# The first layer of experts 1 to 7 as seven block products (Strassen's algorithm, one level)

## The chip, the cores and the metric

The kernel runs on one core of a Trainium2 chip. The core has TensorE (PE, with its weight loads as PEld), VectorE (DVE), ScalarE (ACT), GpSimd (POOL) and SyncE (SP), each with its own queue of instructions. The metric is the time of one execution in device microseconds: 835.72 us, median of three runs (833.84 to 838.47).

## The reference

Attention over a sliding window, then a layer of eight experts, of which each token takes two:

```python
def _attn_ref(q, k, v, n_sink, window):          # 4 batches, 8 heads, 768 positions, 64 wide
    scores = scale * np.matmul(q, k.transpose(0, 1, 3, 2))
    keep = is_sink | in_window                   # 4 sinks, window of 128
    scores = np.where(keep, scores, -1000000000.0)
    a = softmax(scores)
    return np.matmul(a, v)
...
def _moe_ref(x, w_gate, w_noise, noise, w1, w2): # x 3072 x 512, w1 8 x 512 x 1024, w2 8 x 1024 x 512
    noisy_logits = x @ w_gate + np.log1p(np.exp(x @ w_noise)) * noise
    top2, top2_w = the two best experts of each token, and their softmax
    for e in range(E):
        for k in range(2):
            mask = top2[:, k] == e
            h = np.maximum(x[mask] @ w1[e], 0.0)
            out[mask] += top2_w[mask, k, None] * (h @ w2[e])
```

The change is to `x[mask] @ w1[e]`.

## The kernel before

**Numbers.** All is float32. For TensorE a matrix is split into two parts of a narrower type (float32r): a high part, which is a rounded copy written by ScalarE, and a low part, which is the difference and is written by VectorE (`minus`, L191 and L192). One product is three matmuls, high by high, high by low and low by high.

**Order.** A planner (`Plan`, L44) takes every operation with its engine, an assumed duration, a priority and the buffers that it reads and writes. It simulates the engines and writes out one fixed order for each. A tag with a ring of n buffers can be ahead of its readers by n. Phase one is attention of four batches with the routing of each; phase two is the routing of the last batch and then the experts.

**Experts.** Each expert has 832 slots for tokens, in seven tiles: six of 128 and a last one (TF) of 64 (R). Before, an expert is worked in two pieces, tiles 0 to 2 (384 columns) and tiles 3 to 6 (448 columns); expert 0 has 512 and 320. F is 1024, in 8 blocks f of 128. For each piece and each f:

- `up` (L990): twelve matmuls, four blocks of the 512 inputs by three, into a bank H (two of them). These are L997 to L999: w1 is stationary, the tokens stream.
- `up_h` (L1008, ScalarE) writes the rectified high part, `up_l` (L1015, VectorE) the low part.
- `down` (L1018) for each tile of the piece: three matmuls of 512 columns into the tile's bank Y (L1026 to L1028), for the last tile two (L1031, L1032).

So first and second layer alternate, f by f. When a tile's bank Y is complete, ScalarE scales it by the routing weight (L1035; the last tile takes `half`, `whole` and `scaled`), and GpSimd adds it to the output by an indirect DMA (`scatter`, L1048 to L1052, with a one-element memset ahead of it).

**Inputs of an expert.** `w_chunk` (L918) brings each matrix in four chunks of 512 KB: SP loads a chunk into one of two staging buffers `st`, ScalarE writes the high part (L940), VectorE the low part (L944). A chunk of w1 serves two blocks f. `gather` (L825, L838) brings the tokens, 32 rows by each of 26 indirect DMAs of GpSimd into a ring `xg` of five buffers; a gate (`after`) ties gathers to the f of the piece before. `weight` (L964) copies the routing weights, four 32 x 1 copies a tile. `rows_turn` (L868) turns a tile with VectorE's transpose of 32 x 32 blocks (L886) and splits it, high by ScalarE (L895), low by VectorE, into `skn` and `sqn`, two buffers each.

The first layer's matmuls in the kernel before:

```python
for i in range(DC):
    xh, xl = (x[:, i, :width] for x in both)
    nc.tensor.matmul(p, w[:, 0, i], xh, start=(i == 0), stop=False)
    nc.tensor.matmul(p, w[:, 0, i], xl, start=False, stop=False)
    nc.tensor.matmul(p, w[:, 1, i], xh, start=False, stop=(i == DC - 1))
```

## Time and profile before

| | |
|---|---|
| time, median of three runs | 835.72 us |
| profiled execution, span | 836.0 us |
| granted clock of TensorE, mean | 0.990 |
| matmuls in the profile | 4801 |
| `up`, L997 to L999, all experts | 512 each, 541.4 us busy in sum |
| gathers (L838) | 182, 180.6 us of GpSimd |
| scatters (L1050) | 56, 92.0 us of GpSimd |
| data moved | 97.10 MB, mean 116 GB/s |

"Busy" is the time from the start of an instruction to its end, and instructions of one engine that overlap are counted once in the shares but each for itself in the groups. A row of a group reads: line, engine, operation, output <- input, count, then busy time, mean ns of one, then the engine's idle time just before them and what ended it. "Issue" is idle time for which the profile names no releaser. A row of the timeline reads: start, length, engine, line, operation, tile and, in brackets, the wait ahead of it.

### The profile page before, as it was taken

The numbers are of one execution on the slowest core, as the hardware profiler recorded it, in microseconds if no ns is written. First come the engines' busy times: TensorE is split into PE (matmuls) and PEld (weight loads), VectorE is DVE, ScalarE is ACT, GpSimd is POOL, SyncE is SP. The second block draws the span as 40 slices with busy tenths as digits, with TensorE's granted clock in tenths as the row PEclk, the third lists the DMA queues.
The fourth block names the chain that finished last, engine by engine and source line by source line (L and its number), as shares of the span: only waits on it lengthen the run. The fifth ranks groups of instructions, "written<-read, shape, count | busy, mean of one in ns | idle before, by whom it ended". The sixth has DMA issues, their size and how long they took to land.

```text
span 836.0 us, 13410 instructions
## 1 busy us (share of the span) xinstructions
PE 794.0 (95%) x4801; PEld 668.6 (80%) x4801; DVE 442.8 (53%) x1094; ACT 343.5 (41%) x677; POOL 430.3 (51%) x601
## 2 busy tenths in 40 slices
PE   6999997898899799999999999999999999999996
PEld 3776775676677589888988988898899889889984
DVE  5878979888673334346335424633542463454220
ACT  4876785675521323234233323423332341433210
POOL 6555866767416325472753647275364627526212
PEclk9999999999999899999999999999999999999999
DMA  6749886644544186175444617544461654444123
GB/s 120 154 96 226 181 204 183 157 127 100 141 132 131 31 224 165 29 152 120 94 84 127 136 31 153 122 92 84 129 131 35 150 124 94 80 130 78 21 31 47
DMA packets 151750, 97.10 MB, mean 116 GB/s; under 512 B 100704, under 2 KB 129376, under 8 KB 151680
## 3 DMA queue, kind: packets, MB, share of 16 engines
q1 hardware_dynamic: 137744, 67.93, 31.8%
q0 software_dynamic: 13936, 28.27, 19.4%
q8 instruction: 39, 0.64, 0.3%
q14 instruction: 31, 0.25, 0.1%
HBM read 67.44 MB, written 28.72 MB: 115 GB/s over the span
## 4 chain that ended last, share of the span: by engine, by line
PE 75%; issue 7%; DVE 6%; POOL 4%; DMA 4%; ACT 2%; another core or an unknown queue 1%; SPq 1%; POOLq 0%; DVEq 0%; ACTq 0%
PE H L997 10%; PE H L999 10%; PE H L998 10%; PE Y L1026 9%; PE Y L1028 9%; PE Y L1027 9%; PE S L307 4%; PE X L388 2%; PE T L280 2%; PE X L391 2%; POOL out L1050 2%; PE P L365 1%; PE Y L1031 1%; PE Y L1032 1%; DMA st<-in_moe_w 1%
## 5 line engine op out<-in xcount | busy, mean ns | idle before, releaser
L1050 POOL DMA_INDIRECT out<-y,idx x56 | 92.0, 1642 | 241.2 <-ACT y L1035 209.3
L838 POOL DMA_INDIRECT xg<-x_rows,rt_idq x182 | 180.6, 992 | 55.5 <-issue 53.4
L1015 DVE SCALAR_TENSOR_TENSOR h<-H,h 128x384 fp32r<-128x384 f32 (+2 forms) x192 | 79.4, 441 | 219.6 <-ACT h L1008 142.2
L997 PE MATMUL H<-skn,w 128*128 128x448 f32 (+3 forms) x512 | 181.6, 355 | 1.8 <-issue 1.8
L999 PE MATMUL H<-skn,w 128*128 128x448 f32 (+3 forms) x512 | 180.5, 353 | 1.5 <-issue 1.5
L998 PE MATMUL H<-sqn,w 128*128 128x448 f32 (+3 forms) x512 | 179.3, 350 | 1.8 <-issue 1.8
L1008 ACT ACTIVATE h<-H 128x448 fp32r<-128x448 f32 (+3 forms) x128 | 66.1, 516 | 273.7 <-PE H L999 161.8
L997 PEld LDWEIGHTS H<-skn,w 128*128 128x128 f32 x512 | 96.2, 188 | 11.2 <-issue 3.1
L998 PEld LDWEIGHTS H<-sqn,w 128*128 128x128 f32 x512 | 96.3, 188 | 10.6 <-issue 2.4
L999 PEld LDWEIGHTS H<-skn,w 128*128 128x128 f32 x512 | 96.3, 188 | 7.3 <-issue 1.8
L1026 PE MATMUL Y<-w2b,h 128*128 128x512 f32 x192 | 76.0, 396 | 0.3 <-ACT h L1008 0.2
L1028 PE MATMUL Y<-w2b,h 128*128 128x512 f32 x192 | 75.5, 393 | 0.5 <-DVE h L1015 0.5
L1026 PE MATMUL Y<-w2a,h 128*128 128x512 f32 x192 | 75.5, 393 | 0.0
L1027 PE MATMUL Y<-w2b,h 128*128 128x512 f32 x192 | 75.5, 393 | 0.0
L1027 PE MATMUL Y<-w2a,h 128*128 128x512 f32 x192 | 75.0, 391 | 0.0
L1028 PE MATMUL Y<-w2a,h 128*128 128x512 f32 x192 | 74.8, 389 | 0.0
L307 PE MATMUL S<-kq 64*128 64x264 f32 (+1 forms) x384 | 57.4, 410 | 4.4 <-DVE cbuf L317 2.5
L192 POOL TENSOR_TENSOR cbuf<-cbuf,mn 128x528 f32<-128x528 f32 x48 | 51.7, 1077 | 18.4 <-DVE mn L327 16.4
L895 ACT ACTIVATE skn<-xtn 128x512 fp32r<-128x512 f32 (+1 forms) x49 | 29.4, 600 | 68.0 <-DVE xtn L886 55.3
L1028 PEld LDWEIGHTS Y<-w2b,h 128*128 128x128 f32 x192 | 36.3, 189 | 9.9 <-DVE h L1015 1.7
L307 PEld LDWEIGHTS S<-kq 64*128 64x128 f32 x384 | 31.4, 192 | 15.6 <-issue 4.8
L192 DVE TENSOR_TENSOR sqn<-xtn,skn 128x512 fp32r<-128x512 f32 (+1 forms) x49 | 31.9, 652 | 22.1 <-ACT skn L895 16.0
(191 smaller groups left out, 1362.7 us busy)
## 6 DMA issues: line engine op xcount, KB each, us to landing
st<-in_moe_w SPq DMA_DIRECT2D x36, 512.0 KB
st<-in_moe_w SPq DMA_DIRECT2D x112, 128.0 KB
out<-zt SPq DMA_DIRECT2D x31, 256.0 KB
vn<-in_v SPq DMA_DIRECT2D x16, 384.0 KB
x_rows<-xr SPq DMA_DIRECT2D x48, 128.0 KB
kn<-in_k SPq DMA_DIRECT2D x30, 192.0 KB
qn<-in_q SPq DMA_DIRECT2D x30, 192.0 KB
xg<-x_rows,rt_idq POOLq DMA_INDIRECT x182
```

The costliest lines, as they stand in the source:

```text
L192: eng.tensor_tensor(out, a, b, op=OP.subtract)
L307: nc.tensor.matmul(p[:, :2 if j else 1], kq(g)[r, j // 2, 2 + j % 2, NS:], x[:, :2 if j else 1], start=True, stop=True)
L838: nc.gpsimd.indirect_dma_start(out=x[:, i, :], out_offset=None, in_=xbuf.rearrange("r (q d) -> (r q) d", d=sh.SW), in_offset=bass.Indirect ...
L997: nc.tensor.matmul(p, w[:, 0, i], xh, start=(i == 0), stop=False)
L998: nc.tensor.matmul(p, w[:, 0, i], xl, start=False, stop=False)
L999: nc.tensor.matmul(p, w[:, 1, i], xh, start=False, stop=(i == DC - 1))
L1008: nc.scalar.activation(get("h", FC * q + f, [128, 2 * 128 * FIRST], F32R)[:, :width], get("H", FC * q + f), AF.Relu)
L1015: nc.vector.scalar_tensor_tensor(h[:, o:o + s1 - s0], p[:, s0:s1], 0.0, h[:, s0:s1].bitcast(F32), op0=OP.max, op1=OP.subtract)
L1026: nc.tensor.matmul(p, hh, w[:, 0], start=(f == 0), stop=False)
L1027: nc.tensor.matmul(p, hh, w[:, 1], start=False, stop=False)
L1028: nc.tensor.matmul(p, hl, w[:, 0], start=False, stop=(f == FC - 1))
L1050: d = nc.gpsimd.indirect_dma_start(out=out, out_offset=bass.IndirectOffsetOnAxis(ap=c["idx"][:size(e, t), e, t:t + 1], axis=0), in_=get("y ...
```

## The change

Experts 1 to 7 compute the first layer by Strassen's algorithm. Of a pair of blocks f (f0 = 2i and f1 = 2i + 1, with chunk i of w1; i from 0 to 3), the weights are four blocks: the two halves of the 512 inputs by f0 and f1. The tokens are four as well: the halves of the inputs by the halves of the tokens, alternate runs of 32 of the slots, 416 columns each. Instead of eight products of blocks there are seven, a to g, of sums of blocks. Each product is two blocks of 128 inputs by three matmuls, six matmuls of 416 columns. Expert 0 keeps the old way.

```diff
+def split_seven(plan, nc, e, i, n, z):
...
+    def two(b, m, src):
...
+        plan.op("ACT", .06 + .21 * m, z, lambda: nc.scalar.activation(h(), src(), AF.Copy), ...)
+        plan.op("DVE", .06 + .27 * m, z, lambda: minus(v, l(), src(), h().bitcast(F32)), ...)
...
+    two(0, 2, raw)
+    sums(lambda: v.tensor_tensor(extra(), raw(0, 2, 1), raw(2, 4, 1), op=OP.add))
+    sums(lambda: minus(v, raw(0, 2, 1), raw(0, 2), raw(0, 2, 1)))
+    two(6, 1, extra)
+    two(2, 2, lambda: raw(0, 4, 1))
+    sums(lambda: minus(v, raw(0, 2), extra(), raw(0, 2)))
+    sums(lambda: minus(v, raw(2, 4), raw(2, 4), raw(0, 2)))
+    two(4, 2, raw)
...
+def rows_seven(plan, nc, sh, e, t, size, z):
...
+    def sums(o, a, b):
+        plan.op("Pool", .33 * f, z, lambda: minus(gp, o(), a(), b()), w=[raw_])
...
+    plan.op("DVE", .62 * f, z, blocks, r=[("xg", n, j) for j in range(ni)], w=[raw_], u=[("xg", n), ("old", 1)])
...
+    split(0, 2, lambda: raw(0), key(0))
+    sums(...)                                    (four)
+    split(2, 2, lambda: raw(1), key(2))
+    split(4, 2, lambda: extra(0, 4), key(4))
+    split(6, 1, lambda: raw(0, 2, 4), key(6))
...
+    def seven(n, tag, i, a, b, start, stop):
...
+        for k in range(2):
...
+            nc.tensor.matmul(p, wh, h, start=start and not k, stop=False, skip_group_check=True)
+            nc.tensor.matmul(p, wh, l, start=False, stop=False, skip_group_check=True)
+            nc.tensor.matmul(p, wl, h, start=False, stop=k == 1, skip_group_check=True)
...
+    turn = "a0 b0 d0 c0 a1 e0 b1 f0 g0 c1 d1 e1 a2 b2 f1 g1 c2 d2 e2 a3 b3 f2 g2 c3 d3 e3 f3 g3".split()
...
+            product("a", A, 0, 0, True, False)
+            kept(uk)
+            product("b", C, 1, 1)
+            added(f0, 0, uk, C, pc, pc)
+            product("c", A, 4, 5, False, False)
+            kept(uk + 1)
+            product("d", B, 2, 4, True, False)
+            product("e", A, 6, 2, False, False)
+            kept(uk + 2)
+            added(f1, 1, uk + 2, B, pb, lambda k=uk + 2: u_of(k))
+            product("f", A, 5, 3, False, True)
+            product("g", B, 3, 6, False, True)
+            post(f0, 1, pa, [A], zp + 1)
+            added(f1, 0, uk + 1, B, pb, lambda k=uk + 1: u_of(k))
+            op("Pool", .3, zp + 5, lambda f0=f0: again(f0), ...)
```

A product's bank is A (tag H, two buffers), B (tag X, one) or C (tag TX, one). `kept` is a copy of bank A to SBUF by ScalarE, which lies between the products that go on adding to that bank; `added` is a sum by VectorE of another bank and that copy, followed by `post`, the rectified high part (`high`, ScalarE) and the low part (`low`, VectorE). `again` copies 64 columns of the last tile by GpSimd. For one chunk of w1 there are four sums and four splits on VectorE (three of 512 columns, one of 256) and four copies on ScalarE; for one tile of tokens four sums on GpSimd, seven splits of 128 columns on VectorE and seven copies on ScalarE.

The second layer of these experts no longer alternates with the first. It goes tile by tile (`down7`: tile 0, the last tile, then 1 to 5), eight blocks f each, from one region `hb` that holds the high and low parts of the whole expert. Other edits: the ring `xg` falls from five buffers to three and the gate `after` is gone; the ring `y` falls from four to three; w1 is kept in two halves of one region (`wr`) instead of a ring of four; many small tiles of phase two share regions (`Heap`, `lay_out`); chunk 3 of w1 of expert 0 is loaded and split in phase two instead of phase one, by VectorE instead of GpSimd; the buffer for descriptors of GpSimd's DMAs is set:

```diff
-    nc = bacc.Bacc("TRN2", target_bir_lowering=False, num_devices=1)
+    nc = bacc.Bacc("TRN2", target_bir_lowering=False, num_devices=1, dynamic_dma_scratch_size=8192)
```

TensorE before, in the middle of an expert: the end of one `up` (L999), the `down` of the piece's three tiles, and the next `up`.

```order
L999 MATMUL H_6264<-skn_5921,w1_5966 128x384
L1026 MATMUL Y_6204<-w2a_6038,h_6252 128x512
L1027 MATMUL Y_6204<-w2a_6038,h_6252 128x512
L1028 MATMUL Y_6204<-w2a_6038,h_6252 128x512
L1026 MATMUL Y_6212<-w2a_6038,h_6252 128x512
L1027 MATMUL Y_6212<-w2a_6038,h_6252 128x512
L1028 MATMUL Y_6212<-w2a_6038,h_6252 128x512
L1026 MATMUL Y_6219<-w2a_6038,h_6252 128x512
L1027 MATMUL Y_6219<-w2a_6038,h_6252 128x512
L1028 MATMUL Y_6219<-w2a_6038,h_6252 128x512
L997 MATMUL H_6294<-skn_5921,w1_6048 128x384
```

TensorE after, the end of the products of expert 7 (H is bank A, X is bank B; Y are second-layer banks, Y_6074 of tile 0, Y_6120 of the last tile, Y_6140 of tile 1; w2a and w2b are chunks of w2, w2b_6203 the last). "x3" means three such rows in a row. First the end of product d, a piece of second layer and product e:

```order
L1278 MATMUL X_6110<-x7_3924,wr_1791 128x416
L1279 MATMUL X_6110<-x7_3924,wr_1791 128x416
L1280 MATMUL X_6110<-x7_3924,wr_1791 128x416
L1312 MATMUL Y_6120<-w2a_6047,hb_3533 128x512 x2
L1278 MATMUL H_6027<-xe_3381,wr_1791 128x416
```

A second-layer piece of the last tile has moved in between two products. Then the end of product g, the expert's last, and what follows:

```order
L1280 MATMUL X_6110<-x7_3924,wr_1791 128x416
L1309 MATMUL Y_6074<-w2a_6123,hb_3533 128x512 x6
L1309 MATMUL Y_6074<-w2b_6107,hb_3533 128x512 x6
L1312 MATMUL Y_6120<-w2a_6123,hb_3533 128x512 x4
L1312 MATMUL Y_6120<-w2b_6107,hb_3533 128x512 x4
L1309 MATMUL Y_6140<-w2a_6047,hb_3533 128x512 x3
L1309 MATMUL Y_6140<-w2a_6123,hb_3533 128x512 x3
L1309 MATMUL Y_6074<-w2b_6203,hb_3533 128x512 x6
L1312 MATMUL Y_6120<-w2b_6203,hb_3533 128x512 x4
```

In all, thirteen second-layer matmuls (3, 3, 2, 2 and 3) stand between the last products of an expert, all with the first chunk of w2; behind the last product 26 stand ahead of the first that reads the last chunk of w2.

VectorE before, two blocks f of an expert: the two pieces of a low part (L1015), and between them a split of tokens, of w2 or of w1, copies of weights and a transpose.

```order
L1015 SCALAR_TENSOR_TENSOR h_5440<-H_5421,h_5440 128x384
L1015 SCALAR_TENSOR_TENSOR h_5440<-H_5421,h_5440 128x64
L192 TENSOR_TENSOR w1_5444<-st_5391,w1_5444 128x1024
L964 COPY wc1_124<-xg_5376 32x1 x4
L886 STREAM_TRANSPOSE xtn_5485<-xg_5376 128x512
L1015 SCALAR_TENSOR_TENSOR h_5483<-H_5458,h_5483 128x384
```

VectorE after, near the end of the products of expert 7 (L223 is the new line of `minus`, L1296 `total`, L1302 `low`):

```order
L223 TENSOR_TENSOR st_5759<-st_5759 128x2x128
L223 TENSOR_TENSOR w2a_6047<-st_6009,w2a_6047 128x1024
L1296 TENSOR_TENSOR tmp_3505<-X_6000,tmp_3505 128x416
L1296 TENSOR_TENSOR TX_6050<-TX_6050,tmp_3505 128x416
L223 TENSOR_TENSOR wr_1791<-st_5759,wr_1791 128x512
L1302 SCALAR_TENSOR_TENSOR hb_3533<-H_5933,hb_3533 128x13x32
L1302 SCALAR_TENSOR_TENSOR hb_3533<-tmp_3505,hb_3533 128x13x32
```

What stood between two low parts before is one split or a few short rows; now splits of w1 and w2 of 512 and 1024 columns stand in one queue with the sums and low parts of the products, and a sum from bank X (L1296) is what frees that bank for the next product.

More of the change, by code (lines that the diff above doesn't have):

```diff
@@ L37 @@
 ZEROS = 16
+WIDE = 416
 def dram(t, off, ap):
@@ L62, in get @@
         kx = (tag, i)
+        if kx not in self.live and tag in self.laid:
+            return self.laid[tag](i, shape, dt)
         if kx not in self.live:
@@ L862, in halves, with rows_region, first_w, w_region @@
 def halves(plan, sh, i):
-    i += sh.B * sh.H // 2
-    return [plan.get(nm, i, [128, 4, 128 * FIRST], F32R, "early") for nm in ("skn", "sqn")]
+    if not i:
+        both, w = plan.get("xe", 0, [128, 4096], F32R, "early"), 128 * FIRST
+    else:
+        w = CAP - 128 * FIRST
+        both = rows_region(plan)[:, 9216:9216 + 8 * w]
+    return [both[:, 4 * w * j:4 * w * (j + 1)].rearrange("p (c w) -> p c w", c=4) for j in range(2)]
+def rows_region(plan):
+    return plan.get("hb", 0, [128, 8 * (2 * CAP + 64)], F32R, "sb")
+def first_w(plan, i):
+    return w_region(plan)[:, i * 2048:(i + 1) * 2048] if i < 3 else rows_region(plan)[:, 11776:]
+def w_region(plan):
+    return plan.get("wr", 0, [128, 7168], F32R, "early")
 def rows_turn(plan, nc, cst, sh, e, t, size, ring, z):
@@ L979, in experts @@
     FA = sh.FA
-    plan.rings.update(w1=4, w2a=2, w2b=2, skn=2, sqn=2, wc=2, h=FC + 1, y=4, H=2, Y=4, TX=1)
+    plan.rings.update(w1=4, w2a=2, w2b=2, x7=1, hb=1, ws=2, wc=2, raw=4, old=1, u=3, ext=2, h=FC + 1, y=3, H=2, Y=4, TX=1)
     scat = {}
@@ new lines, in experts, with ends @@
+    for tiles in pieces(sh, 0):
+        info.append((0, tiles, sum(size(0, t) for t in tiles)))
+    def ends(e, t, n, z):
+        if size(e, t) == 128:
+            op("ACT", .57, z, lambda: down_c(e, t), r=[("Y", n), ("wc", e, t)], w=[("y", n)],
+               u=[("wc", e), ("old", 1)])
+        else:
+            op("ACT", .5, z, lambda: half(e), r=[("Y", n)], w=[("y", n)], u=[("old", 1)])
+            op("DVE", .6, z, lambda: whole(e), r=[("Y", n)], w=[("y", n)])
+            op("DVE", .6, z, lambda: scaled(e), r=[("wc", e, TF)], w=[("y", n)], u=[("wc", e)])
+        ix = ("idx", int(e > 0 or t >= FA))
+        op("Pool", 1.7, z, lambda: scatter(e, t), r=[("y", n), ix] + [("zero", i) for i in zeros], w=[("o", n)], lat=3)
@@ new lines, in experts @@
+    z = 0
+    for q, (e, tiles, width) in enumerate(info):
+        dz = 12 * (width / 2400 + .016) + DN1 * sum(1 if size(e, t) == 128 else .67 for t in tiles)
+        for t in tiles:
+            if t >= FA:
+                gather(plan, nc, c, sh, xbuf, e, t, -110 + (t - FA) * 7)
+                weight(plan, nc, c, sh, e, t, -100 + (t - FA) * 7)
+                rows_turn(plan, nc, c, sh, e, t, size(e, t), "TX", -100 + (t - FA) * 7)
+        if not q:
+            w_chunk(plan, nc, sh, w1, w2, 0, 1, 3, -60)
+            for i in (2, 3):
+                w_chunk(plan, nc, sh, w1, w2, 0, 2, i, -50)
@@ new lines, in hx, with again, u_of, keep @@
+    def hx(f, x, j):
+        return mine(plan)[:, f, x * (CAP + R):x * (CAP + R) + CAP].rearrange("p (b j s) -> p b j s", j=2, s=32)[:, :, j]
+    def again(f):
+        h = mine(plan)[:, f:f + 2]
+        nc.gpsimd.tensor_copy(h[:, :, CAP:CAP + R], h[:, :, 2 * CAP:].bitcast(F32))
+    def u_of(k):
+        return blocks(get("u", k, [128, WIDE]))
+    def keep(k, src):
+        nc.scalar.activation(u_of(k), src(), AF.Copy)
+    def total(k, src, out):
+        nc.vector.tensor_tensor(out(), src(), u_of(k), op=OP.add)
@@ L1219, in phase_one @@
              r=[("xrow", 3)], w=[("blank", 0)])
-    for i in range(4):
+    for i in range(3):
         w_chunk(plan, nc, sh, w1, w2, 0, 1, i, PR.get("w1", 36) + i, "Pool", [("xrow", 16 + 3 * i)])
@@ L1271, in moe_kernel @@
             plan.run()
-            live = {kx: t for kx, t in plan.live.items() if kx[0] in ("st", "w1", "w2a", "xtn", "ri", "xg", "skn", "sqn")}
+            live = {kx: t for kx, t in plan.live.items() if kx[0] in ("st", "wr", "w2a", "ri", "xg", "xe")}
         sb = both.enter_context(tc.tile_pool(name="msb", bufs=1))
```

314 lines of the change are left out of this document (221 added, 93 removed).

## The prediction

> **What bounds the kernel now.** First the page: its head, the busy shares, four of the rows in 40 slices and the chain that ended last.
>
> ```profile
> span 836.0 us, 13410 instructions
> ...
> PE 794.0 (95%) x4801; PEld 668.6 (80%) x4801; DVE 442.8 (53%) x1094; ACT 343.5 (41%) x677; POOL 430.3 (51%) x601
> ...
> PE   6999997898899799999999999999999999999996
> ...
> DVE  5878979888673334346335424633542463454220
> ...
> PEclk9999999999999899999999999999999999999999
> ...
> PE 75%; issue 7%; DVE 6%; POOL 4%; DMA 4%; ACT 2%; another core or an unknown queue 1%; SPq 1%; POOLq 0%; DVEq 0%; ACTq 0%
> ```
>
> From the 14th slice on TensorE is full at full clock while VectorE is a third to half busy, and three quarters of the chain lie on PE. So the expert stages, which begin there, are TensorE's. The second view is the busy time in stretches of 73 us, each one expert long (columns: length, then PE, PEld, DVE, ACT and POOL, granted clock, DMA share, GB/s):
>
> ```profile
> 387.00:460.00 73.00, 73.00 (x354) 65.07 (x353) 33.05 (x75) 24.61 (x38) 38.15 (x40) 1.00 0.49 107
> ...
> 606.00:679.00 73.00, 73.00 (x355) 65.01 (x354) 32.94 (x75) 24.84 (x39) 38.20 (x40) 1.00 0.49 106
> ```
>
> PE has no gap in them; VectorE works 33, ScalarE 25 and GpSimd 38 of the 73 us. An expert costs what its matmuls cost, and the other three have room, but not without limit. Their starts, from the timeline of TensorE:
>
> ```profile
> 315.44 0.34 PE L997 MATMUL H<-skn,w 128*128 128x384 f32 x1
> ...
> 400.64 0.34 PE L997 MATMUL H<-skn,w 128*128 128x384 f32 x1
> ...
> 402.74 0.40 PE L1026 MATMUL Y<-w2a,h 128*128 128x512 f32 x1
> ...
> 494.84 0.37 PE L997 MATMUL H<-skn,w 128*128 128x448 f32 x1
> ...
> 497.28 0.39 PE L1026 MATMUL Y<-w2b,h 128*128 128x512 f32 x1
> ...
> 752.51 0.34 PE L997 MATMUL H<-skn,w 128*128 128x384 f32 x1
> ...
> 826.02 0.39 PE L1027 MATMUL Y<-w2b,h 128*128 128x512 f32 x1
> ...
> 827.60 0.39 PE L1028 MATMUL Y<-w2b,h 128*128 128x512 f32 x1
> ```
>
> Busy times of matmuls overlap, so their sum says too much, and I go by the distance of starts. Twelve 384-wide matmuls lie between 400.64 and 402.74: 0.175 us each. Twelve 448-wide ones between 494.84 and 497.28: 0.203. Seven steps of 512 between 826.02 and 827.60: 0.226. An expert is 96 of the first, 96 of the second and 160 of the third: 16.8 + 19.5 + 36.1 = 72.4 us, and its measured period is (752.51 - 315.44)/6 = 72.85.
>
> **What goes.** Seven products take 28 x 6 = 168 matmuls of 416 columns where 192 stood with the same mean width. 416 lies halfway between 384 and 448, so 0.189 us each: 31.8 us for the first layer, 67.9 with the second layer, which keeps its 160 matmuls. 24 x 0.189 = 4.54 us less per expert, **31.8 us for seven**.
>
> The Trainium skill (TensorE: Matmul & The Clock Gate, Back-to-back issue gap) gives the isolated gap as N/2.4 + 2.5 ns, 176 ns at 416, and the saving would be 29.5 us; the rows above are some 13 ns slower at each width, and I go by them.
>
> **What comes, and where it lies.** These groups carry the prices (busy us, mean ns of one, idle before):
>
> ```profile
> L1015 DVE SCALAR_TENSOR_TENSOR h<-H,h 128x384 fp32r<-128x384 f32 x112 | 62.2, 555 | 200.9 <-ACT h L1008 126.2 <-issue 74.7
> ...
> L192 DVE TENSOR_TENSOR w<-st,w 128x1024 fp32r<-128x1024 f32 x28 | 34.2, 1222 | 11.0 <-ACT w L940 10.2 <-issue 0.8
> ...
> L886 DVE STREAM_TRANSPOSE xtn<-xg 128x512 f32<-128x512 f32 x42 | 29.9, 712 | 0.6
> ...
> L192 DVE TENSOR_TENSOR sqn<-xtn,skn 128x512 fp32r<-128x512 f32 x42 | 28.9, 690 | 18.7 <-ACT skn L895 12.6 <-issue 5.6
> ...
> L964 DVE COPY wc<-xg 32x1 f32<-32x1 f32 x182 | 25.9, 142 | 5.2 <-DMA xg<-x_rows,rt_idq 3.4
> ...
> L1015 DVE SCALAR_TENSOR_TENSOR h<-H,h 128x64 fp32r<-128x64 f32 x64 | 13.6, 213 | 0.0
> ...
> L940 ACT ACTIVATE w<-st 128x1024 fp32r<-128x1024 f32 x32 | 33.7, 1053 | 6.9 <-DMA st<-in_moe_w 6.9
> ...
> L395 ACT ACTIVATE ps<-X 128x128 fp32r<-128x128 f32 x48 | 13.3, 276 | 30.2 <-PE X L391 30.0
> ...
> L1008 ACT ACTIVATE h<-H 128x448 fp32r<-128x448 f32 x56 | 30.4, 544 | 124.1 <-PE H L999 73.4 <-PE Y L1028 33.9 <-issue 15.2
> ...
> L838 POOL DMA_INDIRECT xg<-x_rows,rt_idq x182 | 180.6, 992 | 55.5 <-issue 53.4 <-DMA xg<-x_rows,rt_idq 1.8 <-DVE wc L960 0.3
> ...
> L1050 POOL DMA_INDIRECT out<-y,idx x56 | 92.0, 1642 | 241.2 <-ACT y L1035 209.3 <-DMA st<-in_moe_w 19.9 <-issue 8.4
> ...
> L1049 POOL MEMSET spacer<- 1x1 f32 x56 | 16.3, 291 | 0.0
> ...
> L192 POOL TENSOR_TENSOR cbuf<-cbuf,mn 128x528 f32<-128x528 f32 x48 | 51.7, 1077 | 18.4 <-DVE mn L327 16.4 <-DVE cbuf L317 0.8 <-DVE ri L345 0.4
> ...
> L192 POOL TENSOR_TENSOR pcbuf<-cbuf,pcbuf 128x32 fp32r<-128x32 f32 x48 | 13.7, 288 | 12.3 <-ACT pcbuf L356 11.3
> ```
>
> VectorE: 690 ns at 512 and 1222 at 1024 make 1.04 ns a column and 0.16 us fixed. Queued instructions overlap:
>
> ```profile
> 498.12 0.69 DVE L1015 SCALAR_TENSOR_TENSOR h<-H,h 128x384 fp32r<-128x384 f32 x2 [2.96 <-ACT h L1008]
> ```
>
> 0.555 + 0.213 took 0.69, so 0.08 less each when queued: 0.21 us at 128 columns, 0.34 at 256, 0.51 at 416, 0.61 at 512, 1.14 at 1024. Per expert: splits of the rows 42 x 0.21 + 7 x 0.13 (64 columns) = 9.7; transposes 6.5 x 0.63 = 4.1; w1 splits and sums 12 x 0.61 + 20 x 0.34 = 14.1; totals and lows behind the products 28 x 0.51 = 14.3; w2 4 x 1.14 = 4.6; weight copies 26 x 0.15 = 3.9; last tile 1.1. Sum **51.8 of 67.9 us**, against 33 of 73 now. ScalarE by the same steps (276 ns at 128, 544 at 448, 1053 at 1024, 0.08 less in a queue): 49 x 0.2 for the rows, 4 x 1.9 for w1, 28 x 0.43 behind the products, 4 x 0.97 for w2, 4.6 at the tiles' ends: 38 us. GpSimd: 26 gathers x 1.29 (992 and 53.4/182 idle) = 33.5; 7 scatters x 1.93 = 13.5; 28 new sums, by the line between 288 at 32 and 1077 at 528 0.44 us at 128 columns, 11.9 in all; 4 copies x 0.3. Sum **60 of 67.9**.
>
> On average all of it lies beside matmuls. By stage it is closer. During the products VectorE has the 14.3, two w1 chunks 7.1, three w2 chunks 3.4, the copies 3.9 and four transposes 2.5: 31.2 us, while TensorE gives 31.8 and 2.9 for the 13 second-layer matmuls slipped in (order of TensorE above), 34.7. So VectorE is 90% taken there, and TensorE waits for it at three joints of an expert: d of a pair overwrites the bank from which VectorE must first add g of the pair before, and only c (1.13 us) stands between. The add takes 0.51, and with the way from engine to engine on both sides c just covers it; whatever stands ahead of it in the queue is exposed. Bounds: 0 where it is first in line; 4.5 us an expert where a 1.14 us instruction stands ahead at each joint and ScalarE's keeps are late by a third of a us as well. I take one queued instruction per joint, **1.5 us an expert, 10.7 in all**, nearest to the mean instruction of that queue.
>
> The queues that this is moved past: SP issues the same loads, but a w1 chunk now stays in one of two staging buffers until its split ends, and w2's four loads come behind chunks 2 and 3. A load and a gather, from the chain in order of time:
>
> ```profile
> 305.22 4.22 DMA st<-in_moe_w
> ...
> 474.52 4.33 DMA xg<-x_rows,rt_idq
> ```
>
> The last w2 chunk needs a load of 4.2, a ScalarE copy of 1.05 and a VectorE split of 1.14 after the one whose buffer it takes, 6.4 us. Beside it lie product g (1.13) and the 26 second-layer matmuls (5.9 us) that the order puts ahead of the first that reads it: hidden, and without that cover up to 6 us an expert. The smaller buffer for GpSimd's descriptors has no row. It costs nothing if four gathers may still be under way (4.33/1.29); if only two may, a gather takes 2.2 us and GpSimd 23 us more an expert. I take 0, since nothing now shows a gather waiting for room (its 0.29 idle is the same at every one), and keep the other end under rival B. Expert 0's last w1 chunk leaves the attention stage, where GpSimd split it, for the routing stage: a ScalarE copy and a VectorE split beside matmuls, 0.
>
> Handover from expert 0 to 1. Now TensorE starves there for itself:
>
> ```profile
> 272.64 0.40 PE L999 MATMUL H<-skn,w 128*128 128x512 f32 x1 [0.44 <-issue]
> ...
> 279.67 0.58 PE L998 MATMUL H<-sqn,w 128*128 128x512 f32 x1 [0.81 <-issue]
> ```
>
> and from GpSimd's:
>
> ```profile
> 257.95 0.95 POOL L838 DMA_INDIRECT xg<-x_rows,rt_idq  x1 [0.31 <-DVE wc L960]
> ```
>
> Six matmuls in 7 us, no engine named. If that does not recur, up to 6 us are gained; but GpSimd, from 257.95 on, must make expert 1's gathers, sums and four scatters, 33.5 + 11.9 + 7.7 = 53 us, to 311, and the last splits follow, against a first product at 315.44 now. Bounds -6 and +6; I take 0. Behind the last matmul (827.60) the same instructions follow: 0.
>
> **Sum** against the profiled execution: 836.0 - 31.8 + 10.7 = **815 us**. Its span is 0.3 above the median of the runs, less than what separates them.
>
> **Rivals.** (A) VectorE sets the pace of the first layer. For it: 90% there, and each of 16 lows follows a ScalarE relu. Against it: ScalarE has slack and runs ahead of a full queue.
>
> ```profile
> 458.85 0.69 DVE L1015 SCALAR_TENSOR_TENSOR h<-H,h 128x384 fp32r<-128x384 f32 x2 [0.77 <-ACT h L1008]
> ```
>
> Such a wait was 0.77; from 0.22 a low (3.5/16) it costs, and at 0.5 it costs 4.5 us an expert: the gain is gone, 836 us.
>
> (B) Slower: GpSimd becomes the bound because its sums and VectorE's splits hold each other up, both reading two tiles of SBUF.
>
> ```profile
> L676 DVE SCALAR_TENSOR_TENSOR rt_c<-lg,rt_c x4: 207/970/1059, 79.4 to 243.1; 128x48 f32<-128x48 f32 x4
> ```
>
> The same small instruction takes 207 ns with GpSimd idle and 970 (median) amid its work. A wait of 0.76 at each of 28 sums makes GpSimd 60 + 21 = 81 us an expert, and 836 + 7 x 8.4 = 895 us. It costs from 0.28 us a sum and is slower than before from 0.46. Against it: the sums stand in the second-layer stage, where VectorE has about 20 of 36 us to do, and a collision lasts only for the rest of one 0.21 us split. The Trainium skill (SBUF — State Buffer, Who interferes with whom) says that a VectorE instruction with two SBUF inputs and a GpSimd instruction that reads SBUF exclude each other; the row agrees.
>
> (C) Everything is hidden and the starved stretch does not recur: 836 - 31.8 - 6 = 798. (D) That the work is not removed: excluded, the order has 168 matmuls per expert.
>
> **How the numbers follow.** Forecast (804 to 822) 0.60; A (822 to 840) 0.20; B 0.08; C 0.12. The range 800 to 834 leaves out B, the end of A and the lower part of C, about 0.17. A measurement can tell about 0.5%, 4 us: faster holds the forecast, C and half of A, 0.82; within it 0.09; slower 0.09.
>
> **What would show it.** Distance of first products of consecutive experts near 69.4 us (67.9: no joint costs; 72.9: A; above 75: B). First-layer steps of 0.189. Waits of TensorE on VectorE or ScalarE near 1.5 us an expert, at bank X; waits on GpSimd none. VectorE near 52, GpSimd near 60 us busy plus issue per expert. Wrong if 128-column instructions of VectorE or GpSimd last longer than priced, or if TensorE's code starves again in another place.

## The result, and the profile after

The kernel after the change takes **911.08 us** (median of four runs, 906.27 to 914.13); the one before, on the same chip, 835.83 (four runs, 833.84 to 838.47). The ratio is 1.090, with a 95% interval of 1.0852 to 1.0948: slower by 9%. The forecast was 815, the range 800 to 834.

The page of the kernel after, its head, busy shares, two of the rows in 40 slices, the chain and four groups (line, engine, operation, output <- input, count, then busy us, mean ns, idle before and what ended it):

```profile
span 906.9 us, 14272 instructions
...
PE 800.9 (88%) x4633; PEld 667.8 (74%) x4633; DVE 625.9 (69%) x1613; ACT 453.0 (50%) x1139; POOL 559.7 (62%) x824
...
PE   6999998988997889987997799879966995999996
...
PEclk8999998999998999998899899989978997899998
...
PE 45%; DVE 23%; POOL 12%; issue 9%; DMA 5%; ACT 3%; SPq 1%; another core or an unknown queue 0%; POOLq 0%; DVEq 0%; ACTq 0%
...
L223 POOL TENSOR_TENSOR turned<-turned 128x128 f32<-128x128 f32 (+1 forms) x196 | 110.3, 623 | 6.4 <-DVE turned L1064 4.4
...
L1287 POOL CAST hb<-hb 128x128 fp32r<-128x128 f32 x28 | 14.8, 530 | 128.2 <-DVE hb L1302 101.0
...
L223 DVE TENSOR_TENSOR x<-turned,xe 128x128 fp32r<-128x128 f32 (+1 forms) x196 | 73.9, 422 | 9.9 <-ACT xe L1079 6.0
...
L1064 DVE STREAM_TRANSPOSE turned<-xg 128x512 f32<-128x512 f32 (+1 forms) x49 | 32.1, 663 | 49.8 <-DMA xg<-x_rows,rt_idq 42.5
```

TensorE's row, full from the 14th slice on before, now has dents in the expert stages, and TensorE holds 45% of the chain instead of 75%. The 168 matmuls that the change removes are gone (4801 - 4633). By stretches of one expert each (first product to first product; the last row is expert 7 to its last matmul; columns as before):

```profile
483.50:569.00 85.50, 73.80 (x329) 64.67 (x328) 61.74 (x152) 42.51 (x107) 59.98 (x76) 0.92 0.44 94
569.00:652.20 83.20, 74.14 (x329) 64.89 (x328) 57.46 (x145) 38.48 (x101) 55.13 (x70) 0.94 0.41 90
...
828.40:898.20 69.80, 69.80 (x335) 62.27 (x333) 28.71 (x50) 27.55 (x49) 15.51 (x22) 1.00 0.40 72
```

Experts 1 to 6 take 83 to 88 us, where 69.4 was forecast and 72.85 was the period before. Expert 7, for which no next expert's tokens are gathered, runs without a gap; VectorE has 28.7 us to do there, half of what it has in the others. The loss lies between the products: from expert 1's first product to expert 7's, 18 distances of more than 1.2 us between the starts of two matmuls make 69 us (66 beyond the pace), and matmuls at distances of 0.28 to 1.2 us, where 0.19 or 0.23 is the pace, another 36. One such gap, from the timeline (start, length, engine, line, operation, tile, wait and what ended it):

```profile
683.06 0.35 PE L1280 MATMUL X<-x,wr 128*128 128x416 f32 x1
683.39 0.94 POOL L873 DMA_INDIRECT xg<-x_rows,rt_idq  x1 [0.30 <-issue]
...
685.88 0.94 POOL L873 DMA_INDIRECT xg<-x_rows,rt_idq  x1 [0.30 <-issue]
686.69 0.52 ACT L1299 ACTIVATE hb<-H 128x416 fp32r<-128x416 f32 x1 [2.41 <-remote]
687.11 1.14 ACT L1024 ACTIVATE wr<-st 128x512 fp32r<-128x512 f32 x2
687.24 0.59 DVE L1302 SCALAR_TENSOR_TENSOR hb<-H,hb 128x416 fp32r<-128x416 f32 x1 [2.18 <-issue]
688.83 0.59 DVE L1296 TENSOR_TENSOR tmp<-X,tmp 128x416 f32<-128x416 f32 x1 [0.99 <-remote]
...
689.48 0.71 PE L1278 MATMUL X<-x,wr 128*128 128x416 f32 x1 [6.06 <-DVE tmp L1296]
```

TensorE waits for VectorE, VectorE for ScalarE, and ScalarE for something that the view can only call "remote". It is TensorE itself: the trace lists each engine's semaphore updates, and the one for the last matmul into H, which ended at 682.26, stands at 686.67; the one for the matmul that ends at 683.06 + 0.35 stands at 688.80. ScalarE starts 0.02 us behind the first, VectorE 0.03 behind the second. GpSimd issues gathers the whole time, 1.25 us apart.

Other gaps are of another kind. The longest of them, 7.25 us from 491.96 on:

```profile
497.88 0.71 DVE L1064 STREAM_TRANSPOSE turned<-xg 128x512 f32<-128x512 f32 x1 [8.56 <-DMA xg<-x_rows,rt_idq]
498.52 0.55 DVE L1302 SCALAR_TENSOR_TENSOR hb<-TX,hb 128x416 fp32r<-128x416 f32 x1
499.21 0.69 PE L1278 MATMUL TX<-xe,wr 128*128 128x416 f32 x1 [6.90 <-DVE hb L1302]
```

Here no update is late. VectorE stands at a transpose until a gather has landed, and the low part that frees TensorE's bank stands behind it. Of the 69 us, six gaps with 31 are of this kind. In seven with 29, a waiting engine's releaser is "remote", or several updates of TensorE come at once after a silence, as in the gap above. The other five, 9 us, are neither.

### The profile page after: what moved, and what is told of

Same layout as the page of the kernel before. It is cut to its first block, busy times and chain, and to the rows that moved or that the text cites. A ratio compares the mean times of both kernels' runs of the same rounds, so it can differ in the third digit from the quotient of the medians.

```text
span 906.9 us, 14272 instructions
## 1 busy us (share of the span) xinstructions
PE 800.9 (88%) x4633; PEld 667.8 (74%) x4633; DVE 625.9 (69%) x1613; ACT 453.0 (50%) x1139; POOL 559.7 (62%) x824
## 4 chain that ended last, share of the span: by engine, by line
PE 45%; DVE 23%; POOL 12%; issue 9%; DMA 5%; ACT 3%; SPq 1%; another core or an unknown queue 0%; POOLq 0%; DVEq 0%; ACTq 0%
DVE x L223 8%; PE Y L1309 7%; POOL xg L873 6%; PE S L340 4%; POOL out L1202 4%; PE H L1278 3%; PE H L1280 3%; PE H L1279 3%; PE X L421 2%; DVE wr L223 2%; PE X L1278 2%; PE X L1280 2%; PE P L398 2%; DMA st<-in_moe_w 2%; PE X L424 2%
## 5 line engine op out<-in xcount | busy, mean ns | idle before, releaser
L1309 PE MATMUL Y<-w2a,hb 128*128 128x512 f32 x504 | 126.3, 391 | 0.0
L1309 PE MATMUL Y<-w2b,hb 128*128 128x512 f32 x504 | 124.5, 390 | 0.0
L223 POOL TENSOR_TENSOR turned<-turned 128x128 f32<-128x128 f32 (+1 forms) x196 | 110.3, 623 | 6.4 <-DVE turned L1064 4.4
L1309 PEld LDWEIGHTS Y<-w2b,hb 128*128 128x128 f32 x504 | 94.6, 188 | 18.9
L1309 PEld LDWEIGHTS Y<-w2a,hb 128*128 128x128 f32 x504 | 94.5, 188 | 18.5 <-issue 0.4
L1278 PE MATMUL H<-xe,wr 128*128 128x416 f32 x168 | 65.7, 391 | 31.2 <-ACT tmp L1293 17.0
L1202 POOL DMA_INDIRECT out<-tmp,idx x37 | 66.9, 1809 | 34.1 <-ACT tmp L1187 22.1
L1279 PE MATMUL H<-x,wr 128*128 128x416 f32 x224 | 83.7, 374 | 0.0
L223 DVE TENSOR_TENSOR x<-turned,xe 128x128 fp32r<-128x128 f32 (+1 forms) x196 | 73.9, 422 | 9.9 <-ACT xe L1079 6.0
L1293 ACT ACTIVATE tmp<-H 128x416 f32<-128x416 f32 x84 | 42.8, 515 | 70.1 <-PE H L1280 36.5
L223 DVE TENSOR_TENSOR wr<-st,wr 128x512 fp32r<-128x512 f32 x84 | 58.7, 703 | 12.4 <-ACT wr L1024 11.6
L1064 DVE STREAM_TRANSPOSE turned<-xg 128x512 f32<-128x512 f32 (+1 forms) x49 | 32.1, 663 | 49.8 <-DMA xg<-x_rows,rt_idq 42.5
L223 POOL TENSOR_TENSOR cbuf<-cbuf,mn 128x528 f32<-128x528 f32 x48 | 52.2, 1089 | 19.8 <-DVE mn L360 18.3
L1280 PE MATMUL H<-xe,wr 128*128 128x416 f32 x168 | 62.6, 373 | 0.0
```

Source lines behind the costliest of these rows:

```text
L223: eng.tensor_tensor(out, a, b, op=OP.subtract)
L1064: v.transpose(turned().rearrange("p i c s -> p (i c s)"), x)
L1202: d = nc.gpsimd.indirect_dma_start(out=out, out_offset=bass.IndirectOffsetOnAxis(ap=c["idx"][:size(e, t), e, t:t + 1], axis=0), in_=get("y ...
L1278: nc.tensor.matmul(p, wh, h, start=start and not k, stop=False, skip_group_check=True)
L1279: nc.tensor.matmul(p, wh, l, start=False, stop=False, skip_group_check=True)
L1280: nc.tensor.matmul(p, wl, h, start=False, stop=k == 1, skip_group_check=True)
```

## The experiments

Two theories at the start. **T**: the planner's assumed durations are too short, gathers land late, and VectorE and GpSimd wait in order for each other. **V**: VectorE's work and its collisions with GpSimd's sums set the pace. Later **P**: long runs of gathers hold TensorE's signals back. Chips differ: the kernel before takes 836 to 839 us on some (the result above, and all runs below but seven) and 828 on others. Each number stands beside the kernel before on the same chip. One without an interval is a single run; the four runs of the changed kernel above spread over 8 us, and on another chip it took 921.

### One part of the change undone (before: 838.77)

The copy `again` from GpSimd to ScalarE, the order otherwise kept:

```diff
-        nc.gpsimd.tensor_copy(h[:, :, CAP:CAP + R], h[:, :, 2 * CAP:].bitcast(F32))
+        nc.scalar.activation(h[:, :, CAP:CAP + R], h[:, :, 2 * CAP:].bitcast(F32), AF.Copy)
```

> The copy `again` is issued by ScalarE instead of GpSimd, at the same place of the program; the orders of VectorE and TensorE and of the rest of GpSimd stay as in the changed kernel (911 us). Theory T (GpSimd and VectorE wait for one another in turn: gathers stand behind `again`, which waits for low parts; low parts and sums of VectorE stand behind transposes that wait for gathers): the 17 us an expert that GpSimd stands ahead of `again` go to gathers, periods of experts 1 to 6 fall from 86 to 73 to 79 us, time 835 to 870. Rival V (VectorE's work, made longer by collisions with GpSimd's sums, sets the pace): periods stay at 83 or more, time 895 to 915.

**941.54 us**, further from the forecast than the change itself. GpSimd no longer waits for VectorE there, so that its gathers run closer together, 14 in a run instead of 13, and TensorE's gaps beside them grow to 10 to 14 us. Both theories miss.

The sums of the tokens from GpSimd to VectorE, order kept:

```diff
-        plan.op("Pool", .33 * f, z, lambda: minus(gp, o(), a(), b()), w=[raw_])
+        plan.op("Pool", .33 * f, z, lambda: minus(v, o(), a(), b()), w=[raw_])
```

> The four sums of each tile of tokens are issued by VectorE instead of GpSimd, at the same place of the program. GpSimd loses 24 x 0.6 = 15 us an expert, VectorE gains some 26 x 0.2 = 5 and loses its collisions, 0.26 at about 22 of its splits, 6 us. T (GpSimd's lateness is what counts): gathers come up to 15 us earlier, time 835 to 875, though `again` still stands in GpSimd's queue. V: VectorE's load is the same, time 900 to 920; were the collisions alone at fault, VectorE's 128-column splits fall from 0.36 to 0.28 us and the time by 6 x 6 us to 875.

**934.75 us.** No sum collides any more, and it is slower. Both theories miss again; VectorE does the sums besides its own work here, so this run alone doesn't clear it.

Gathers of experts 1 to 7 replaced by plain loads of fixed rows, issued by SP. This leaves the routing of the rows out; the amounts moved and the arithmetic stay:

```diff
-        nc.gpsimd.indirect_dma_start(
-            out=x[:, i, :], out_offset=None, in_=xbuf.rearrange("r (q d) -> (r q) d", d=sh.SW),
-            in_offset=bass.IndirectOffsetOnAxis(ap=cst["idq"]()[:, i, n:n + 1], axis=0))
+        nc.sync.dma_start(x[:, i, :], xbuf.rearrange("r (q d) -> (r q) d", d=sh.SW)[1024 + 128 * i:1152 + 128 * i, :])
```

> The gathers of experts 1 to 7 become plain loads of as many bytes from fixed rows, issued by SP at the same place of the program (the routing of the rows is left out, so the output is of other tokens). GpSimd loses 26 x 1.29 = 34 us an expert; sums, collisions and all of VectorE's, ScalarE's and TensorE's work stay. T: VectorE no longer waits for gathers (10 us an expert at transposes), periods 69 to 74, time 805 to 845. V: periods of 83 or more, time 890 to 915. If loads of rows stand behind loads of weights in SP's queue, part of the waits stays.

**826.34 us**, 0.985 of before. VectorE's work is all there, three experts by the windows:

```profile
376.60:451.90 75.30, 70.38 (x329) 62.78 (x329) 57.65 (x147) 38.48 (x101) 30.07 (x46) 0.98 0.46 108
451.90:527.00 75.10, 71.07 (x329) 62.58 (x328) 60.28 (x150) 42.44 (x107) 31.92 (x49) 0.98 0.47 110
527.00:597.40 70.40, 68.82 (x330) 61.36 (x329) 56.93 (x147) 38.74 (x102) 28.96 (x44) 1.00 0.44 103
```

VectorE does its 57 to 60 us in 70 to 75, far from the 83 and more that V said. So V is out as the main cause, and the gathers on GpSimd are in it. No signal of TensorE is late in this trace. But the six periods of experts 1 to 6 are 74.9 us on average, more than the 72.85 before the change: what this run gains lies ahead of expert 1 (first product at 297.8) and in expert 7. TensorE still waits for ScalarE and VectorE between the products, 25 us in 12 gaps; the three longest, 11 us, stand behind transposes that wait for rows, which now come late from SP's queue.

Then T's remedy: the planner's durations set to the measured ones (a sum on GpSimd .64, a split of tokens .36, a weight copy .143, a scatter 2.1, and so on):

```diff
-        plan.op("Pool", .33 * f, z, lambda: minus(gp, o(), a(), b()), w=[raw_])
+        plan.op("Pool", .64, z, lambda: minus(gp, o(), a(), b()), w=[raw_])
...
-    plan.op("DVE", .065 * (size // 32 if e else 1), z, go, ...)
+    plan.op("DVE", .143 * (size // 32 if e else 1), z, go, ...)
```

> The work of the changed kernel, but the planner is given the durations that its profile showed (sums of GpSimd 0.64 instead of 0.33 us, scatters 2.1 instead of 1.7, splits of tokens on VectorE 0.36 instead of 0.2, weight copies 0.57 instead of 0.26 a tile, and so on); it then plans periods of 74 to 77 us where it planned 69 to 70. T, in the form that the plan's durations put transposes too early in VectorE's queue: the time comes near to that plan, 6 x 75 + 79 instead of 597 us for experts 1 to 7, 835 to 860. If GpSimd or VectorE have not enough time whatever the order is: 885 or more.

**895.39 us.** What T named is cured: VectorE's transposes (from 320 us on) no longer wait for gathers.

```profile
L1064 DVE STREAM_TRANSPOSE turned<-xg 128x512 f32<-128x512 f32 x36 | 25.1, 702 | 0.1
```

The time, 895, is what was expected if GpSimd or VectorE lacked time in any order. The trace shows something else: the experts still take 81 to 86 us, with one gap of 9 us in each of four, such as

```profile
507.02 0.71 PE L1278 MATMUL H<-xe,wr 128*128 128x416 f32 x1 [8.73 <-ACT tmp L1293]
```

where TensorE's updates for matmuls that ended between 496 and 498.3 stand at 499.99, 503.55 and 506.43, beside a run of gathers. Hence P, and the question of the gate that the change took away.

### The gate (before: 827.94 on a chip of the other kind, 839.16 on one of the first)

The kernel before without its gate, nothing else changed:

```diff
-                gather(plan, nc, c, sh, xbuf, e, t, zt - 10, after)
+                gather(plan, nc, c, sh, xbuf, e, t, zt - 10)
```

> The kernel before, without the gate `after` that ties each gather to the f of the piece before; the planner then puts up to 20 gathers in one run on GpSimd, the work is the same. Theory P (gathers issued back to back hold back the signals of TensorE's finished matmuls by up to 9 us, so that ScalarE and VectorE start late and then TensorE waits; seen in the last runs where three updates of TensorE arrive within 0.2 us, 9 us after the matmuls): such late groups of updates appear once or more per expert, 3 to 9 us each of which the two banks H hide a part, time 850 to 890. Theory T (late gathers in front of VectorE's sums): gathers come earlier than before and nothing waits for them, time 825 to 842.

**830.01** against 827.94: nothing. The changed kernel with a gate, each gather tied to a step of TensorE in the expert before, 2.0 us apart by the planner's figures:

```diff
+        def paced(t, i, e=e):
+            x = 0 + 2.0 * (4 * t + i)
+            return [("step", e - 1, int(x / P7) if x < up7 else 28 + int((x - up7) / DN1))]
-            gather(plan, nc, c, sh, xbuf, e, t, z0 - 60 + 3 * t)
+            gather(plan, nc, c, sh, xbuf, e, t, z0 - 60 + 3 * t, paced if e > 1 else None)
```

> The changed kernel with a gate again: gather k (0 to 25) of an expert waits for that matmul group of the expert before which is planned 2.0 us x k after its first product; durations of the planner, work and rings stay. P: no more runs of gathers, TensorE's updates come at once, stalls of 20 us an expert fall under 6, periods 70 to 76, time 815 to 855. T alone: gathers come later than in the changed kernel (911), transposes and what is behind them wait as long or longer, 900 to 940.

**844.59** (1.020). And with it the gate at 1.8 and durations between the old and the measured ones:

> As the gate before, at 1.8 us, and the planner's durations nearer to the profile (sums of GpSimd 0.52 us, scatters 2.1, splits of tokens 0.25, weight copies 0.62 a tile, `again` 0.5). P and T together: the transposes stand where their gathers have landed, and TensorE's updates are not held: periods 69 to 73, time 805 to 835. P alone: as the kernel with the gate only, within 10 us.

**850.36** (1.027). In four experts (470 to 770 us) its product stages are nearly unstalled (37.6 us for 36.1 of matmuls), and the second layer now waits for the low parts of w2, 14 us in the four. No update of TensorE is late on this chip, in any of the three. So the null result of the first was tied to the chip, not to the gate, and the next three ran on a chip of the first kind: the changed kernel again, the same with the 2.0 us gate, and a version with the sums on VectorE, splits of tokens joined to 256 columns and the gate at 1.8.

> The changed kernel unchanged, as the control on the same chip as the next two. In the runs with the gate no update of TensorE was late and the kernel before took 828 instead of 836 to 839 us, so part of the effect may be the chip's. Theory T (gathers late against a plan with too short durations, transposes ahead of sums in VectorE's queue): 890 to 915 on any chip, 1.07 to 1.09 of the kernel before. Theory P (updates of TensorE held back amid gathers): 1.03 to 1.05 on a chip where they are not held.

> The changed kernel with the gate at 2.0 us, as before, beside its control: 1.02 of the kernel before by T, whatever the chip does to updates, since a gate also takes runs of gathers away.

> Gate at 1.8 us, the durations nearer to the profile, the sums of tokens on VectorE (no collisions with GpSimd, which loses 15 to 19 us an expert, so scatters and the tile ends on ScalarE are not late), and two neighbouring splits of tokens in one instruction of 256 columns (28 splits an expert instead of 49). VectorE has 56 us of 70 to do. T: periods 69 to 72 us, 805 to 830, 0.97 to 1.00 of the kernel before. If VectorE's load or its order is the bound after all: periods of 74 or more, 840 or more.

**921.26** (1.098), **857.60** (1.022) and **839.99** (1.001) against 839.16. Two experts in the middle of each, by the windows; first the changed kernel again:

```profile
481.30:570.70 89.40, 75.66 (x329) 65.82 (x328) 61.68 (x152) 42.39 (x107) 58.33 (x77) 0.90 0.43 91
570.70:659.30 88.60, 75.11 (x330) 65.57 (x329) 57.43 (x145) 38.33 (x101) 53.50 (x69) 0.90 0.38 84
```

the same with the gate:

```profile
461.90:539.60 77.70, 71.46 (x330) 62.21 (x329) 59.27 (x148) 40.49 (x104) 58.93 (x74) 0.98 0.46 100
539.60:615.70 76.10, 71.15 (x329) 62.37 (x328) 58.90 (x148) 40.32 (x104) 58.10 (x74) 0.98 0.47 102
```

and the version without GpSimd's sums:

```profile
464.40:538.30 73.90, 70.28 (x330) 62.61 (x329) 56.48 (x155) 38.94 (x83) 44.90 (x45) 0.98 0.50 107
538.30:611.70 73.40, 70.58 (x329) 62.51 (x328) 56.32 (x155) 38.62 (x83) 42.71 (x45) 0.98 0.49 105
```

The gate alone, with the same work on every engine, takes 64 us off. From expert 2 on, gathers then come in runs of 8 at most; without it in runs of 12 and 13, with 7 to 10 us of gaps beside each. It takes off waits of both kinds: with it the transposes don't wait for gathers any more either (41.8 us without it):

```profile
L1064 DVE STREAM_TRANSPOSE turned<-xg 128x512 f32<-128x512 f32 x36 | 25.5, 709 | 0.3
```

So the 64 us can't all be put down to P. The last version's periods are 69.7 to 78.8 us, 74.5 on average. That and its time are what was expected if VectorE's load or its order were the bound after all (74 or more, 840 or more).

What the gate leaves shows in the second of the three. In each of four experts, TensorE stands still for some 4 us in the products:

```profile
544.17 0.35 PE L1280 MATMUL X<-x,wr 128*128 128x416 f32 x1
547.06 0.69 ACT L1187 ACTIVATE tmp<-Y,wc 128x512 f32<-128x512 f32 x1 [3.94 <-DMA out<-tmp,idx]
547.64 0.51 ACT L1293 ACTIVATE tmp<-H 128x416 f32<-128x416 f32 x1
548.21 0.55 PE L1278 MATMUL H<-x,wr 128*128 128x416 f32 x1 [3.68 <-ACT tmp L1293]
```

ScalarE's copy of bank A (L1293) stands behind the scaling of a finished tile (L1187), and that waits for a scatter to leave its buffer of the ring `y`, which the change cut from four to three. In the kernel before, ScalarE never waits for a scatter from 311 to 773 us. The same four gaps are there on the other kind of chip (844.59), where no update is late. A version with four buffers was not run.

### Is it the gate, or what the gate goes with? (before: 838.44)

The last version with `again` on VectorE and the gate at 2.0, the last version without the gate, the changed kernel with the gate at 1.3 us, and, on this kind of chip, the kernel before without its gate:

> As the kernel with gate, sums on VectorE and merged splits (840 us, 1.00 of the kernel before), but with the gate at 2.0 us and `again` on VectorE (0.3 us four times an expert), so that GpSimd never stands ahead of low parts. T and P: the stalls that end on `again` or behind scatters go (some 2 us an expert), those of 3 to 4 us at bank B in the middle of the products get rarer; periods 70 to 73, 818 to 838, 0.975 to 1.00 of the kernel before. If VectorE's queue sets the pace: 840 or more.

> The kernel of 840 us without its gate: sums on VectorE, merged splits, durations near to the profile, but the gathers in runs as in the changed kernel. T (late gathers against too short durations and a full GpSimd): both causes are gone, within 10 us of 840. P (runs of gathers hold back TensorE's updates): 865 to 900, with groups of late updates in the trace.

> The changed kernel with the gate at 1.3 us instead of 2.0, which is the pace of gathers issued back to back, but tied to TensorE's progress. P: the gathers lie as close as without a gate, 880 to 915. T: a gather that is tied to progress cannot fall behind the plan by more than its own wait, 845 to 870, as with 2.0 (858).

> The kernel before without its gate once more, beside the others of this call: on a chip on which the kernel before takes 836 to 839 us, P expects 850 or more, T 832 to 842 (it was 830 beside 828 on a faster chip, without a late update in the trace).

**867.33** (1.0324, interval 1.0276 to 1.0371), **886.14**, **907.91** and **917.47**. The last one settles it: the old kernel, with its own work, loses 79 us when only its gate goes, and its transposes wait for no gather. From 337 us on its gathers come in runs of 18 (the first of 23), and beside each of five runs TensorE stands still, once for 14 us and four times for 9 to 10, from the 13th or 14th gather on:

```profile
447.68 0.94 POOL L838 DMA_INDIRECT xg<-x_rows,rt_idq  x1 [0.30 <-issue]
448.39 0.43 PE L999 MATMUL H<-skn,w 128*128 128x384 f32 x1 [0.38 <-issue]
...
452.67 0.94 POOL L838 DMA_INDIRECT xg<-x_rows,rt_idq  x1 [0.30 <-issue]
456.93 0.87 ACT L1008 ACTIVATE h<-H 128x384 fp32r<-128x384 f32 x2 [16.50 <-remote]
457.47 0.80 PE L1026 MATMUL Y<-w2b,h 128*128 128x512 f32 x1 [8.65 <-ACT h L1008]
```

The matmul ended at 448.82; TensorE's update for it stands at 456.86, and 0.07 us later ScalarE starts. In between no engine but GpSimd does anything, and the DMA engines are a fifth busy (window, length, PE, PEld, DVE, ACT, POOL, clock, DMA share):

```profile
449.00:457.00 8.00, 0.00 (x0) 0.00 (x0) 0.00 (x0) 0.07 (x1) 3.70 (x4) 0.59 0.19 44
```

The version without gate (886.14) has VectorE's waits for gathers back (25 us at transposes) and 5 to 6 us of gaps beside its runs of 11 and 12. The first one, with the gate, was meant to be the best and lost 27 us to the version before it: its gathers come in runs of 11, closer together than in that one, and each of five runs has 5.4 to 6.2 us of gaps behind the 8th gather, with late updates. Whether `again` gone from GpSimd or the other pace of the gate made the runs closer was not tested. The gate at 1.3 us lets runs of 11 and 14 through, and there TensorE also waits 28 us for the low parts of w2.

### Spacing instead of a gate (before: 827.58, a chip of the other kind)

The kernel before without its gate but with two GpSimd memsets behind each gather, the version of 839.99 with `again` on VectorE and four short ones (with the gate, and without), and the kernel before without its gate as a control:

```diff
             in_offset=bass.IndirectOffsetOnAxis(ap=cst["idq"]()[:, i, n:n + 1], axis=0))
+        nc.gpsimd.memset(cst["filler"], 0.0)
+        nc.gpsimd.memset(cst["filler"], 0.0)
```

> The kernel before without its gate, with two memsets of 128x512 (0.55 us each) behind each gather on GpSimd, which has the room: as many gathers, in the same order, but 2.3 to 2.4 us apart instead of 1.25. P (the pace of a run of gathers holds TensorE's signals back, from about the 13th gather of a run on): no stalls, within 8 us of the kernel before. If it is the number of gathers under way or their place in the order, not their pace: as without memsets, beside this in the same call (917 on an earlier chip).

> The changed kernel with gate at 1.8 us, sums and `again` on VectorE, merged splits, durations near to the profile, and four memsets of 128x64 behind each gather (0.5 to 0.6 us together), so that gathers lie 1.8 us or more apart. P: no held signals; periods 69.5 to 72, 0.965 to 0.99 of the kernel before. If runs at 1.8 us still hold signals: 1.00 to 1.03 as before.

> The same without the gate: runs of gathers at 1.8 us. If the pace alone decides, within 8 us of the one with gate; if the length of a run decides too, 850 or more (886 without gate and without memsets).

> The control of the first of this call: the kernel before without its gate. P on a chip of the more frequent kind: 900 to 930; on a chip where nothing is held: within 5 us of the kernel before, and then the first run of this call tells nothing.

**903.62**, **874.43** (1.058, interval 1.0546 to 1.0613), **865.37** and **832.20** (1.006). They fell on a chip on which nothing is held back, so they say nothing of spacing as a remedy. The control has runs of 18 gathers at the same 1.25 us, and from expert 1's first product on TensorE has not one gap; a window of 18 us amid such a run:

```profile
398.00:416.00 18.00, 18.00 (x92) 16.33 (x91) 3.38 (x11) 2.95 (x7) 13.43 (x16) 1.00 0.23 56
```

The memsets made GpSimd itself the bound: in the first of the four it is busy 70.6 of 80 us and the experts wait for it.

```profile
440.00:520.00 80.00, 74.14 (x346) 65.80 (x345) 32.10 (x74) 23.81 (x38) 70.59 (x97) 0.96 0.43 99
```

The third, without gate, shows that late gathers cost time where no signal is held too: VectorE's copies and transposes wait for them, and the kernel takes 38 us more than before. Its memsets make the gathers later than they would be without.

```profile
L1119 DVE COPY wc<-xg 32x1 f32<-32x1 f32 x182 | 26.0, 143 | 52.7 <-DMA xg<-x_rows,rt_idq 50.1
L1067 DVE STREAM_TRANSPOSE turned<-xg 128x512 f32<-128x512 f32 x42 | 29.6, 705 | 17.6 <-DMA xg<-x_rows,rt_idq 13.0 <-issue 4.5
```

## Why the prediction was wrong

**The removal was right.** 24 x 7 matmuls are gone, first-layer steps are 0.189 to 0.191 us apart, and expert 7, which nothing disturbs, takes 69.8 us to its last matmul.

**The joints, and rival A.** The joints were put at 1.5 us an expert, 10.7 in all. Expert 7 has 0.3 us of gaps in its products, but with 28.7 us of work on VectorE it does not test them. Where VectorE has its full load, 57 to 62 us in experts 2 to 6 instead of the 51.8 worked out, the price depends on the order. With the gate and longer durations the products lose 1.5 us, as forecast; but there the second layer waits 3.5 us an expert for low parts of w2, which the prediction took to be hidden. Without gathers, periods are 74.9 us on average, and 74.5 in the version that ties. Both lie above A's sign, 72.9, though not by A's mechanism, since VectorE is busy for only 56 to 60 of them. No version brought experts 1 to 6 below the 72.85 of before on average, so in none of them did the saving of 31.8 us come through. The handover from expert 0, put at 0, gave 3.8 us (first product at 311.6 instead of 315.4).

**The step that failed** is the one on the queues that work is moved past. It weighed SP's loads and the smaller buffer for descriptors, and it gave the gate `after`, which the change removes, no term at all. What the gate does in the kernel before is keep gathers in runs of 10 or 11 from expert 1's second piece on. Without it, the kernel before loses 79 us, by held signals; the changed kernel takes 64 more than with a gate, by held signals and late gathers; the forecast was missed by 96. Between the two numbers stands a remainder of some 30 us, which the gate does not give back: with it TensorE still has 26 us of long gaps and some 20 of slow matmuls. Of the 26, 15 are the four gaps behind a scatter, so the shorter ring `y`, which had no term either, is the first suspect; that was not tested by itself.

**The row that showed it had been quoted.** Between 272.64 and 279.67 TensorE makes six matmuls in 7 us, with no engine named. The prediction took that for a matter of the handover that might not recur. The gathers of expert 1's first piece have no gate in the kernel before either, and that stretch lies in their run of 18: it was the one place in the old trace where the effect could be seen. No update of TensorE stands between 266.24 and 279.69, then four within 1 us. The runs on the other kind of chip settle that it is the same effect. There the same gathers come at the same pace (254 to 276 us, in the kernel before without its gate), no update is late, and TensorE has no gap. First the kernel before in the profile that the prediction quotes, then that one (832.20):

```profile
268.00:282.00 14.00, 8.88 (x30) 6.12 (x29) 2.42 (x9) 1.99 (x4) 6.76 (x8) 0.79 0.16 40
268.00:282.00 14.00, 14.00 (x71) 12.06 (x70) 6.92 (x20) 6.11 (x11) 11.07 (x13) 1.00 0.24 51
```

In the two runs of that kernel on such chips, expert 1's first product comes at 308.9 and 311.0 instead of 315.4. So 4 to 6 of the 8 us between the two kinds of chip lie ahead of expert 1, where this stretch is.

**GpSimd's sums were mis-sized.** They were put at 0.44 us and take 0.62. VectorE's splits of tokens were put at 0.21 in a queue and take 0.36 to 0.39 at 128 columns. With GpSimd's sums gone and the rest kept (934.75) they take 0.28. First the changed kernel, then that one:

```profile
L223 DVE TENSOR_TENSOR x<-turned,xe 128x128 fp32r<-128x128 f32 x144 | 50.2, 393 | 0.0
L223 DVE TENSOR_TENSOR x<-turned,xe 128x128 fp32r<-128x128 f32 x146 | 36.4, 282 | 3.9 <-ACT xe L1079 3.9
```

So rival B's mechanism is real. These rows agree with the Trainium skill's rule on two-input VectorE instructions and GpSimd reads (SBUF — State Buffer, Who interferes with whom). But the bound that B forecast is not what was found, and B's 895 us, close to the result, would have been right for a wrong reason: with the sums moved away the time is 934.75 without the gate and in the old order, 886.14 without it in a new one.

**T holds for a part.** In the changed kernel VectorE waits 42.5 us for gathers at its transposes, and GpSimd 101 at `again` for VectorE. Longer durations remove the first and leave 895; the gate alone removes it too and leaves 858; both, with the sums on VectorE, 840. Gap by gap, late gathers and held signals share the changed kernel's long gaps about evenly (31 and 29 us of 69). How much each costs by itself does not follow from that, since a held signal makes VectorE late, and a late VectorE delays gathers.

**What stays open.** Why some chips hold TensorE's signals back isn't known. On those chips the trace also lacks some update records when gathers run on GpSimd: the kernel before without its gate has 632 of TensorE's on one of them and 657 on each of two of the others, and the changed kernel has 1032 of ScalarE's for 1119 instructions. The version without gathers, on such a chip, has all 1119. So the recording itself may have a part in the effect, and no run without recording is here to tell. The changed kernel as it is was not run on a chip of the other kind; with the gate it takes 1.020 there and 1.022 here. No version that does all the work is faster than the kernel before: the best ties, 1.001 in a single run.

## What to carry to other kernels

A dependency that looks like mere pacing can be what keeps a queue's bursts short: when a change drops one, ask how long the runs on that queue become, and look in the old trace for the one place where they already were that long. A stage that has lost most of its work on the other engines, as expert 7 here, does not test whether the matmuls of the other stages stay fed. A gap between two matmuls of the same kind can have different causes, so follow each of the long ones back before a total is put down to one. A wait of several microseconds whose releaser the profile can't name, beside a run of gathers, is worth checking against the producer's own end time before an engine is blamed. And an effect that comes with the chip can make the decisive experiment read as null, so run the control beside it on the chip that showed the loss.
